# Loading and converting the first layer's weights earlier in a fused attention and two-layer expert kernel

## The chip, the cores and the metric

The kernel runs on one core of a Trainium2 chip. The time is device microseconds of one execution, and the result is the median of a few executions. Before the change it is 835.37 us (three runs, 835.11 to 836.59).

## What is computed

Three stages follow one another; 2176 tokens pass through all of them.

```python
# attention: 4 batches, 8 heads, 512 local and 32 global queries of 64 numbers
s_ll = where(abs(i - j) <= 32, scale * q_l @ k_l.T, -1e9)      # band of local keys
out_l = softmax([scale * q_l @ k_g.T, s_ll]) @ [v_g, v_l]
out_g = softmax(scale * q_g @ [k_g, k_l].T) @ [v_g, v_l]
x = [out_g, out_l] as rows of 512                               # 2176 x 512
# dense layer
h = x @ w_in                                                    # 512 x 2048
x = (h * sigmoid(h)) @ w_out                                    # 2048 x 512
# experts: tokens shared out over 8 experts by a capacity rule, then
out[mask] = relu(x[mask] @ w1[e]) @ w2[e]
```

The array w_in holds 64-bit floats. The kernel reads them as pairs of 32-bit words and makes 32-bit floats of them on the chip.

## The kernel before

The tokens are cut into six units (UNITS): the first has 256 tokens, the others 384. For units 0 to 3 the kernel computes attention and, mixed with it on TensorE, the matrix product with w_in of the unit whose attention is already done. Units 4 and 5 and the later stages come after that, and the change doesn't touch them.

**Attention** is a list of ticks (TICKS): a transpose of a chunk of keys (step_k, L250 and L256), of global rows (step_g, L262 to L267) or of queries (step_q, L250 and L272), a block of local attention (local, for batch b, query block qb and half hh of the heads, written (b, qb, hh) below), or global attention (glob). One call of piece() runs a tick, and with it the next stage of the attention blocks that are under way. A local block goes through scores on TensorE (L354, L359), row maxima on DVE (L371), exponentials on ACT (L378), transposes on TensorE (L385), a copy on ACT (L387), the product with V on TensorE (L392), scaling on DVE (L395), a transpose back on TensorE (L401), and then the two halves of x, the high part on ACT (L404) and the low part on DVE (L406).

**The weights** w_in come in 16 chunks of 128 columns, w0 to w15, 512 KB each (w_in_chunk, a generator that stops between its steps). A chunk is loaded by SP (L84). Its conversion takes two instructions on ACT (L68, L70), three on DVE (L72, L73, L74), one on POOL (L75), the cast of the high part on ACT (L94) and the low part on POOL (L96). All of these stand in the queues of engines that also serve attention, in program order. The class Line keeps the chunks: load() issues the next one's load, step() takes the chunks that are under way one step further and begins the next.

**The order** is set by hand in piece(). Each call adds a rate to wl, and chunks are loaded until the chunk count reaches wl; each call also adds a rate to acc[0], and for every whole unit there win.step() is called. Before unit 0's matrix product has begun (begun is empty) the rates are 0.26 and 0.25, from then on 0.4 and 0.4, and the steps only begin after four calls. Attention's own loads are issued in the order of the list LOADS by load_ahead(n), which runs up to six loads ahead of the ticks. Ahead of everything else load_ahead(6) issues the first six. Unit 0's matrix product (unit_dram, mm_h, L523) starts when both 128-token blocks of the unit are done, and the calls of piece() go on between its matmuls.

All loads named here are issued by SP on one queue, apart from the first batch's global rows, which ACT issues.

Of the kernel before, what the change touches and what calls it, by code (L numbers as in the profile page):

```python
# [27 lines left out]
def tile_kernel(ctx, tc, q_l, k_l, v_l, q_g, k_g, v_g, w_in, w_out, w_gate, w1, w2, out):  # L28
# [434 lines left out]
    def load_ahead(n):  # L463
        while loaded[0] < min(n, len(LOADS)):
            f, *a = LOADS[loaded[0]]
            uses = () if f == load_n and a[1] else USES[f]
            if any(free[u] < uses.count(u) for u in uses):
                return
            for u in uses:
                free[u] -= 1  # L470
            f(*a)
            loaded[0] += 1

    def owed():
        while acc[0] >= 1:
            acc[0] -= 1
            win.step()
# [29 lines left out]
    def ticks():  # L507
        for t in TICKS:

            while t[0] == "L" and through[0] < 2 and 4 * t[1] + t[2] >= 8 + 3 * through[0]:  # L510
                yield "wait"
            yield from tick(t)
        while live:
            yield from advance()
# [35 lines left out]

    T = ticks()
    win = Line()
    load_ahead(6)
    made = [0] * 16
    wl = -0.5
    done = 0
    acc = [0.0, 0.0]
    begun = []

    def piece():  # L560
        nonlocal done, wl
        if next(T, "end") in ("end", "wait"):
            return False
        done += 1
        if done > 4:
            acc[0] += 0.4 if begun else 0.25
            owed()
        wl += 0.4 if begun else 0.26
        while win.at < wl:
            win.load()  # L570
            if win.at == 16: wl = 0
        return True
# [4 lines left out]
    for u in range(RES[0]):  # L577
        while not ready(u):
            piece()
        if u == 0:  # L580
            win.have(0)
            begun.append(1)
        for i, _ in enumerate(unit_dram(u)):
            if u == 0 and i % 4 == 3 and i < 63:
                win.have(i // 4 + 1)
            acc[1] += 0.64 if u == 0 else 0.7
            while acc[1] >= 1 and piece():
                acc[1] -= 1
        through[0] += 1
    while piece():  # L590
        pass
# [702 lines left out]
    done = 0  # L1294
# [57 lines left out]
```

## Time and profile before

| | us |
|---|---|
| median of three runs | 835.37 |
| the profiled execution, its own time | 836.36 |
| its span, first to last instruction | 834.6 |
| TensorE (PE) busy in the span | 796.2 |
| DVE, ACT, POOL busy | 420.4, 391.6, 223.9 |

The profile is of a single execution, some 1 us above the median. PE is busy for 95% of the span, so over the whole kernel PE is what counts, and its 38 us of idle time are what a change of order alone can reach. The page's slices of 20.9 us show where PE isn't busy: in the first four it stands at 6, 6, 9 and 6 tenths, and in nearly all of the others at 9 tenths or more. The first four slices are attention of the first batch, with the conversion of w_in and unit 0's product in it.

### The profile page before, as it was taken

What the parts mean: (1) busy time and instruction counts of PE and PEld (TensorE: products, weight loads), DVE (VectorE), ACT (ScalarE), POOL (GpSimd) and SP (SyncE); (2) the same over time, 40 slices, a digit from 0 to 9 for tenths busy, and PEclk for the clock granted to TensorE, in tenths of its full rate; (3) what the DMA queues carried; (4) which work ended last, traced back from release to release, by engine and by line L of the source; (5) the groups of instructions that cost most, each with busy time, mean ns of one, the idle gap of its engine ahead of it and who ended that gap; (6) DMA issues with size and microseconds to landing.
All of it is one profiled execution on the core that took longest, in us unless ns stands there. A gap on an engine that the chain in (4) does not pass through costs nothing. (4 is left out here: it accounts for less than half of the span.)

```text
span 834.6 us, 18246 instructions
## 1 busy us (share of the span) xinstructions
PE 796.2 (95%) x7407; PEld 671.4 (80%) x7407; DVE 420.4 (50%) x923; ACT 391.6 (47%) x879; POOL 223.9 (27%) x209
## 2 busy tenths in 40 slices
PE   6696999999999999999999999999799999999997
PEld 4475778888888999976667777777589999999994
DVE  3789544544454356520004444566635666666650
ACT  3676544354453466636442434454225454544531
POOL 2456300000000046534243444343230211122001
PEclk9799899999999999999999999999899999999999
DMA  9957853882871443126642325445135656666511
GB/s 177 238 175 206 208 141 95 196 204 76 184 204 40 162 135 115 51 95 197 202 139 64 123 67 187 160 150 174 53 89 170 219 169 226 193 221 205 193 61 38
DMA packets 131687, 125.24 MB, mean 150 GB/s; under 512 B 64560, under 2 KB 100416, under 8 KB 131600
## 3 DMA queue, kind: packets, MB, share of 16 engines
q1 hardware_dynamic: 126912, 114.65, 48.2%
q0 software_dynamic: 2784, 8.93, 3.0%
q8 instruction: 60, 0.98, 0.5%
q10 hardware_dynamic: 1904, 0.46, 0.4%
q14 instruction: 27, 0.22, 0.1%
HBM read 92.68 MB, written 20.71 MB: 136 GB/s over the span
## 5 line engine op out<-in xcount | busy, mean ns | idle before, releaser
L1150 PE MATMUL acc<-w,ghi 128*128 128x512 f32 x544 | 179.6, 405 | 4.3 <-PEq L1034 4.3
L523 PE MATMUL S<-xhi,w 128*128 128x384 f32 (+1 forms) x512 | 167.2, 359 | 0.3 <-DMA h_d<-hs 0.3
L1150 PEld LDWEIGHTS acc<-w,ghi 128*128 128x128 f32 x544 | 101.4, 190 | 32.5 <-issue 11.9
L1150 PE MATMUL acc<-w,glo 128*128 128x512 f32 x272 | 109.8, 404 | 0.0
L1260 PE MATMUL h<-xshi,we 128*128 128x272 f32 x512 | 108.7, 292 | 0.0
L523 PEld LDWEIGHTS S<-xhi,w 128*128 128x128 f32 x512 | 95.4, 191 | 11.0 <-issue 5.5
L58 DVE TENSOR_TENSOR we<-eraw,we 128x1024 fp32r<-128x1024 f32 x64 | 79.8, 1247 | 28.3 <-ACT we L55 28.3
L1278 PE MATMUL acc<-hh,we 128*128 128x272 f32 x448 | 93.4, 288 | 0.0
L58 POOL TENSOR_TENSOR glo<-ht,ghi 128x512 fp32r<-128x512 f32 x44 | 61.8, 1416 | 95.8 <-ACT ghi L55 92.2
L523 PE MATMUL S<-xlo,w 128*128 128x384 f32 (+1 forms) x256 | 83.5, 326 | 1.6 <-DVE xlo L406 1.6
L1260 PEld LDWEIGHTS h<-xshi,we 128*128 128x128 f32 x512 | 84.2, 188 | 0.1
L1260 PE MATMUL h<-xslo,we 128*128 128x272 f32 x256 | 73.8, 288 | 0.0
L1278 PEld LDWEIGHTS acc<-hh,we 128*128 128x128 f32 x448 | 73.7, 188 | 0.0
L523 PE MATMUL h<-xhi,w 128*128 128x384 f32 x256 | 69.7, 341 | 0.7 <-DVE fold L604 0.7
L55 ACT CAST we<-eraw 128x1024 fp32r<-128x1024 f32 x64 | 66.8, 1044 | 0.0
L1264 ACT ACTIVATE hh<-h 128x272 fp32r<-128x272 f32 x64 | 25.4, 398 | 88.0 <-PE h L1260 87.3
L1278 PE MATMUL acc<-hl,we 128*128 128x272 f32 x224 | 64.5, 288 | 0.0
L1150 PEld LDWEIGHTS acc<-w,glo 128*128 128x128 f32 x272 | 51.6, 190 | 14.4 <-issue 2.8
L75 POOL TENSOR_TENSOR cvu<-cvu,cvv 128x512 int32<-128x512 int32 x32 | 41.0, 1283 | 81.3 <-DVE cvu L74 54.6
L1217 POOL DMA_INDIRECT out_dram<-orow,idx x17 | 17.1, 1006 | 158.2 <-DVE orow L1225 140.6
L1166 ACT COPY x<-acc 128x512 f32<-128x512 f32 x17 | 10.0, 587 | 92.6 <-PE acc L1150 91.8
L523 PEld LDWEIGHTS S<-xlo,w 128*128 128x128 f32 x256 | 49.3, 193 | 1.8 <-DVE xlo L406 1.8
(229 smaller groups left out, 1431.6 us busy)
## 6 DMA issues: line engine op xcount, KB each, us to landing
eraw<-in_moe_w_dram SPq DMA_DIRECT2D x64, 512.0 KB, 3.7
ht<-h_d SPq DMA_DIRECT2D x44, 256.0 KB, 3.5
h_d<-hs SPq DMA_DIRECT2D x24, 384.0 KB, 3.3
gh<-h_d SPq DMA_DIRECT2D x12, 768.0 KB, 4.6
w<-in_moe_w_in_dram SPq DMA_DIRECT2D x16, 512.0 KB, 5.4
wraw<-in_moe_w_out_dram SPq DMA_DIRECT2D x16, 512.0 KB, 3.6
V<-vn SPq DMA_DIRECT2D x24, 256.0 KB, 3.8
x_d<-x SPq DMA_DIRECT2D x17, 256.0 KB, 2.0
```

The source lines that it names most:

```text
L55: nc.scalar.copy(hi, src)
L58: eng_lo.tensor_tensor(lo, src, hi.bitcast(F32), op=OP.subtract)
L75: nc.gpsimd.tensor_tensor(u, u, v, op=OP.add)
L523: nc.tensor.matmul(ps[:, :n], a, x[:, cc, :n], start=k == 0, stop=k == 11)
L1150: nc.tensor.matmul(ps, a[:, f % 4], x, start=f == 0 and k == 0, stop=f == 15 and k == 2)
L1166: nc.scalar.copy(x2, ps)
L1217: nc.gpsimd.indirect_dma_start(out=out, out_offset=bass.IndirectOffsetOnAxis(ap=at, axis=0), in_=r[:n], in_offset=None)
L1260: nc.tensor.matmul(ps, a, XS[e][x][:, c, o], start=k == 0, stop=k == 11)
L1264: nc.scalar.activation(hh, ps, AF.Relu)
L1278: nc.tensor.matmul(ACC[i][d], a, x, start=f == 0 and k == 0, stop=f == 7 and k == 2)
```

## The change

The first chunk of w_in is loaded after four of attention's loads and not after six. The counter wl starts at 1.0 in place of -0.5, the steps begin after two calls of piece() and not after four, and the four rates go from 0.25, 0.26, 0.4 and 0.4 to 0.33, 0.32, 0.42 and 0.42.

```diff
     T = ticks()
     win = Line()
+    load_ahead(4)
+    win.load()
     load_ahead(6)
     made = [0] * 16
-    wl = -0.5
+    wl = 1.0
     done = 0
...
         done += 1
-        if done > 4:
-            acc[0] += 0.4 if begun else 0.25
+        if done > 2:
+            acc[0] += 0.42 if begun else 0.33
             owed()
-        wl += 0.4 if begun else 0.26
+        wl += 0.42 if begun else 0.32
         while win.at < wl:
             win.load()
```

What the instructions are stays the same, and on PE their order too. What moves are the 16 loads on SP and the steps of the conversions on ACT, DVE and POOL. Three places show how.

On SP, at the start of the program: raw are attention's keys (L165) and queries (L170), vn and V0, V1 its values, and w0, w1, ... the chunks. Before:

```order
L165 DMA raw_127<-in_k_l_dram 128x8x64
L165 DMA raw_129<-in_k_l_dram 128x8x64
L170 DMA raw_136<-in_q_l_dram 128x8x64
L189 DMA vn_138<-in_v_l_dram 128x8x64
L203 DMA V0_117<-in_v_l_dram 32x8x64 x3
L84 DMA w0_160<-in_moe_w_in_dram 128x4x256
L165 DMA raw_162<-in_k_l_dram 128x8x64
L170 DMA raw_172<-in_q_l_dram 128x8x64
L189 DMA vn_138<-in_v_l_dram 128x8x64
```

With the change:

```order
L165 DMA raw_127<-in_k_l_dram 128x8x64
L165 DMA raw_129<-in_k_l_dram 128x8x64
L170 DMA raw_136<-in_q_l_dram 128x8x64
L84 DMA w0_138<-in_moe_w_in_dram 128x4x256
L189 DMA vn_140<-in_v_l_dram 128x8x64
L203 DMA V0_117<-in_v_l_dram 32x8x64 x3
L84 DMA w1_156<-in_moe_w_in_dram 128x4x256
L165 DMA raw_164<-in_k_l_dram 128x8x64
L170 DMA raw_174<-in_q_l_dram 128x8x64
L84 DMA w2_183<-in_moe_w_in_dram 128x4x256
L189 DMA vn_140<-in_v_l_dram 128x8x64
```

The third chunk of keys now has two chunks of w_in ahead of it and not one, and the second load of values has three and not one. Further on, w3 and w4 stand where w1 and w2 stood.

On ACT, ahead of the exponentials of block (0, 1, 0), which are the two L378 rows. Before:

```order
L68 ACTIVATE cvu_321<-w1_246 128x512
L70 ACTIVATE cvv_322<-w1_246 128x512
L404 CAST xhi_313<-tp_373 128x2x128
L378 ACTIVATE P_365,su2_121<-S_345,st_366 128x128 x2
L378 ACTIVATE P_365,su2_121<-S_346,st_366 128x128 x2
L94 CAST w0_411<-cvu_267 128x512
```

With the change:

```order
L94 CAST w0_329<-cvu_250 128x512
L68 ACTIVATE cvu_335<-w2_183 128x512
L70 ACTIVATE cvv_336<-w2_183 128x512
L404 CAST xhi_325<-tp_387 128x2x128
L94 CAST w1_393<-cvu_298 128x512
L68 ACTIVATE cvu_399<-w3_263 128x512
L70 ACTIVATE cvv_400<-w3_263 128x512
L378 ACTIVATE P_381,su2_121<-S_361,st_382 128x128 x2
L378 ACTIVATE P_381,su2_121<-S_362,st_382 128x128 x2
```

The exponentials stood behind chunk w1's first step; now they stand behind w3's.

On DVE, around the second chunk of the second batch's keys (L256) and that batch's global rows (L264, L267). Before:

```order
L256 COPY kT_114<-tp_1150 128x4x2x2x32
L406 TENSOR_TENSOR xlo_744<-tp_1167,xhi_743 128x2x128
L395 TENSOR_TENSOR x_1195<-tp_1178,st_1024 128x256
L72 TENSOR_SCALAR cvu_1142<-cvu_1142 128x512
L73 TENSOR_SCALAR cvu_1142<-cvu_1142 128x512
L74 SCALAR_TENSOR_TENSOR cvu_1142<-w13_1050,cvu_1142 128x512
L264 COPY gT_1227<-tp_1222 128x256
L267 COPY kT_114<-gT_1227 128x4x8x32
L545 COPY hs_1165<-S_1158 128x2x128
L406 TENSOR_TENSOR xlo_744<-tp_1238,xhi_743 128x2x128
L72 TENSOR_SCALAR cvu_1204<-cvu_1204 128x512
```

With the change:

```order
L256 COPY kT_114<-tp_1174 128x4x2x2x32
L72 TENSOR_SCALAR cvu_1149<-cvu_1149 128x512
L73 TENSOR_SCALAR cvu_1149<-cvu_1149 128x512
L74 SCALAR_TENSOR_TENSOR cvu_1149<-w15_988,cvu_1149 128x512
L406 TENSOR_TENSOR xlo_783<-tp_1196,xhi_782 128x2x128
L395 TENSOR_TENSOR x_1224<-tp_1207,st_1063 128x256
L264 COPY gT_1248<-tp_1243 128x256
L267 COPY kT_114<-gT_1248 128x4x8x32
L545 COPY hs_1194<-S_1187 128x2x128
L406 TENSOR_TENSOR xlo_783<-tp_1259,xhi_782 128x2x128
L371 TENSOR_REDUCE st_1309<-S_1288 128x2
```

Thirteen conversions stood ahead of this L256 on DVE and three behind it; now fifteen stand ahead and one behind.

## Rows read from the trace of the kernel before

**Rows 1.** Stretches: length, PE, PEld, DVE, ACT, POOL busy, PEclk, DMA share, GB/s

```profile
0.00:20.00 20.00, 13.07 (x167) 9.18 (x168) 7.44 (x18) 7.93 (x24) 4.30 (x24) 1.00 1.02 178
20.00:40.00 20.00, 12.15 (x234) 8.64 (x231) 14.88 (x36) 12.70 (x41) 7.28 (x7) 0.83 1.14 247
40.00:60.00 20.00, 18.95 (x261) 14.62 (x260) 16.24 (x36) 14.73 (x39) 12.69 (x10) 0.91 0.52 148
60.00:80.00 20.00, 15.10 (x230) 12.46 (x229) 19.51 (x39) 13.33 (x40) 13.01 (x10) 1.00 0.75 213
80.00:100.00 20.00, 16.42 (x248) 13.92 (x247) 13.50 (x28) 10.21 (x31) 10.53 (x9) 0.83 0.88 211
100.00:140.00 40.00, 40.00 (x587) 32.51 (x587) 18.33 (x60) 18.49 (x69) 1.04 (x2) 1.00 0.52 133
```

**Rows 2.** Waits of PE, 20 to 100 us: total, times, longest (us)

```profile
PE S L359 <- ACT qT L272: 4.2, 2, 3.6
PE tp L385 <- ACT P L378: 3.2, 2, 3.0
PE tp L401 <- DVE x L395: 2.1, 3, 1.3
PE S L354 <- DVE xlo L339: 2.0, 1, 2.0
PE tp L262 <- DVE kT L256: 1.2, 1, 1.2
```

**Rows 3.** Timeline of ACT, 24 to 26 us: start, us, instruction, idle before

```profile
24.60 0.66 ACT L68 ACTIVATE cvu<-w 128x512 f32<-128x512 f32 x1 [4.75 <-DMA w<-in_moe_w_in_dram]
25.16 0.65 ACT L70 ACTIVATE cvv<-w 128x512 int32<-128x512 uint32 x1
25.70 0.36 ACT L404 CAST xhi<-tp 128x256 fp32r<-128x256 f32 x1
25.95 0.38 ACT L378 ACTIVATE P<-S,st 128x128 f32<-128x128 f32 x1
```

**Rows 4.** DMA issues from 20.0 to 20.2 us (chunk w2): size, us to landing

```profile
w<-in_moe_w_in_dram SPq DMA_DIRECT2D x1, 512.0 KB, 6.2
```

**Rows 5.** Timeline of PE, places where it waited

```profile
14.96 1.08 PE L250 MATMUL tp<-ident,raw 128*128 128x128 f32 x4 [1.36 <-DMA raw<-in_k_l_dram]
...
64.83 0.27 PE L354 MATMUL S<-mb,identb 128*128 128x256 bf16 x1 [2.01 <-DVE xlo L339]
...
78.56 0.46 PE L262 MATMUL tp<-ident,raw 64*128 64x64 f32 x4 [1.23 <-DVE kT L256]
...
85.47 1.11 PE L359 MATMUL S<-kT,qT 64*32 64x128 f32 x32 [3.58 <-ACT qT L272]
```

**Rows 6.** Timeline of DVE, 39 to 82 us

```profile
39.32 0.42 DVE L406 TENSOR_TENSOR xlo<-tp,xhi 128x256 fp32r<-128x256 f32 x1
...
77.82 0.68 DVE L256 COPY kT<-tp 128x512 f32<-128x512 f32 x1
...
79.08 0.52 DVE L72 TENSOR_SCALAR cvu<-cvu 128x512 f32<-128x512 f32 x1
...
81.68 0.42 DVE L264 COPY gT<-tp 128x256 f32<-128x256 f32 x1
```

**Rows 7.** Timeline of POOL at 82 us

```profile
81.90 1.26 POOL L75 TENSOR_TENSOR cvu<-cvu,cvv 128x512 int32<-128x512 int32 x1 [1.15 <-DVE cvu L74]
```

**Rows 8.** Timeline of ACT, 83 to 86 us

```profile
83.20 0.62 ACT L94 CAST w<-cvu 128x512 fp32r<-128x512 f32 x1 [1.81 <-POOL cvu L75]
...
84.85 0.57 ACT L272 ACTIVATE qT<-tp 128x512 f32<-128x512 f32 x1
```

**Rows 9.** Single microseconds, columns as in rows 1

```profile
64.00:65.00 1.00, 0.17 (x1) 0.00 (x0) 0.97 (x3) 1.00 (x7) 0.00 (x1) 1.00 1.11 302
84.00:85.00 1.00, 0.00 (x0) 0.00 (x0) 1.00 (x3) 1.00 (x3) 0.92 (x2) 0.68 0.52 125
90.00:91.00 1.00, 1.00 (x6) 1.00 (x6) 0.93 (x3) 0.00 (x0) 0.00 (x0) 0.50 1.06 242
```

## The prediction

> **What bounds the kernel now.** I read the busy time by stretch first, then the waits of PE, then the timelines around the longest of them. The stretches [rows 1] say where anything can be won. From 100 us to 140 us PE is busy all 40.00 us, and from there on it stays so but for the seams between stages. From 20 to 100 us it is busy for 62.6 us of 80 (12.15 + 18.95 + 15.10 + 16.42). DVE is busy for 16.24 of 20 us between 40 and 60 us, and for 19.51 of 20 between 60 and 80. So for 40 us the first unit's stage is bound by DVE, or by ACT and POOL where a conversion hands over to them, and PE waits for their results [rows 2]: 3.6 us in one piece for queries that ACT makes, 3.0 for exponentials, 2.0 before a local block's second score tile, 1.2 for keys. In no row of these waits is PE held by a chunk of w_in. The chunks come in time; what they do is stand in front of attention's work in the queues of ACT, DVE and POOL.
>
> The change leaves PE's instructions and their order as they are. The conversions are the same sixteen. So the whole effect is how much sooner or later PE gets through the attention that is mixed with unit 0's product, that is, through the last long wait, which ends at 85.47 us [rows 5]. From there on PE waits for nothing before 140 us worth counting, and a shift at this point reaches the end in full. The sum has three terms up to that point and one behind it.
>
> **Term 1, the loads: +3.5 us.** Up to 40 us the DMA engines are full: their share stands at 1.02 and 1.14 [rows 1]. Each chunk that is put ahead of attention's loads holds these back by its own length, 524 KB at the 178 or 247 GB/s of these two rows, 2.9 or 2.1 us. The first place where that shows is the third chunk of keys, for which PE waited 1.36 us up to 14.96 us [rows 5]: one more chunk lies ahead of it, so that wait grows by some 2 us. The second place takes that delay in and is longer. ACT stood idle for 4.75 us until w1 landed, at 24.60 us [rows 3], and block (0, 1, 0)'s exponentials came at 25.95. With the change w3 stands at this place. All that lay ahead of w2 in the old queue, and w2 itself, lies ahead of w3 in the new one. w2 was issued at 20.0 to 20.2 us and landed 6.2 us later [rows 4], at 26.3. One chunk more at 2.1 us gives 28.4. From the start of L68 to the next instruction behind L70 it is 1.10 us (24.60 to 25.70) [rows 3], so the exponentials start at 29.5, 3.5 us later than before. I take 247 GB/s, since it is the rate of the stretch in which w3 lands. The bounds: at 178 GB/s +4.4; with the extra chunk at no cost, 26.3 + 1.1 = 27.4, or +1.4. A gain is excluded, because w3 can't land before the bytes that were ahead of w2.
>
> The Trainium skill gives, on its page "DMA: Bandwidth & Descriptors", section "Anatomy of one DMA", a variable cost of bytes over 436 GB/s; by that a chunk would take an estimated 1.2 us and this term would be +2.6. The trace's full engines at 178 and 247 GB/s speak against that rate here.
>
> **Term 2, what DVE makes up: -2.8 us.** Block (0, 1)'s last low part (L406) ran at 39.32 us and the copy of the second batch's second chunk of keys (L256) at 77.82 [rows 6]. Ahead of that L406 DVE has now done six conversions and not four; ahead of that L256 fifteen and not thirteen. Between the two it is nine in either kernel, and the other work is the same, so the 3.5 us are carried along unless DVE's idle time shrinks. That is 3.76 us from 40 to 60 and 0.49 from 60 to 80 [rows 1], 4.25 in all, and it bounds the term from 0 to -4.25. Most of it lies soon after the restart, in waits for results of PE and ACT; with two chunks more in hand, some work is always ready there. I take two thirds, which puts L256 at 77.82 + 3.5 - 2.8 = 78.5 us.
>
> On this stretch a new wait appears. Ahead of the row maxima of block (0, 3, 0) DVE now does a conversion more. Its price is the one from 79.08 to 81.68 us, 2.6 us [rows 6], and PE's wait before L354 at 64.83, now 2.01 us [rows 5], grows by about that. PE gets it back before 78.56, where it waited 1.23 us for L256, and on the way, where it waited for x [rows 2]. So I cost it at nothing; uncovered it would be 2.6 us.
>
> **Term 3, the tail of the conversions: -1.25 us.** From L256 (77.82) to PE's L359 (85.47) it took 7.65 us. In between, ACT's cast of w13 (83.20) waited for POOL's step (81.90, 1.26 us), which waited for DVE, and w15's first step stood between that cast and the queries (84.85) [rows 6 to 8]. With the change only w15's conversion is left there. The chain is L256 0.68, a conversion on DVE 2.60, from its end to the cast 1.52 (81.68 to 83.20), the cast 0.62, a high part (L404) 0.36, and from the queries' start to L359 0.62 (84.85 to 85.47): 6.40 us. L359 comes at 78.5 + 6.4 = 84.9 us, 0.55 us earlier than before.
>
> **Term 4, the clock: -1.4 us.** The granted clock, 1.00 until 84 us, falls to 0.68 in the slice from 84 to 85 and stands at 0.50 until 91 [rows 9], which is the 1.2 GHz level. Behind the 2.01 us wait at 64.83 it stayed at 1.00 [rows 5, 9]; behind the 3.58 us wait it fell. PE worked from 85.47 to 91 at half speed, which cost (91 - 85.47) / 2 = 2.8 us. With the change the wait before L359 is split, a part of it lying before L401, and each part should be under 2 us. Then the clock stays up and 2.8 us are won. But the longer wait before L354 can bring a fall of its own. I take half.
>
> Sum: 3.5 - 2.8 - 1.25 - 1.4 = -1.95 us. The profiled execution would take 836.36 - 1.95 = 834.4; the median of the runs lies 1.0 us lower, so the forecast is **833.4 us**.
>
> **Rivals.**
> *Slower.* The loads cost term 1 and nothing is made up, since DVE was bound by the chain from ACT through POOL and not by its own work. It decides if L256 comes later than about 79.1 us (77.82 + 1.25): then L359 is late. With no idle time made up and the clock as before, +3.5 - 1.25 = +2.25, 837.6 us; at 178 GB/s 838.5. For it speaks that DVE is all but full from 60 to 80 us; against it the 3.76 us of idle time before.
> *No change.* The gains and the delay cancel. L359 comes 0.55 us earlier, and the half-speed stretch moves to the new wait before L354, its cost the same: 834.8 us. The Trainium skill says on "TensorE: Matmul & The Clock Gate", section "What's actually happening", that the low clock is the default and activity releases it; by that the fall follows the longest gap wherever it is put, and the time is this one. The trace agrees so far that the 3.58 us gap brought a fall and the 2.01 us gap none.
> *Twice the gain.* The early loads have room after all (term 1 at +1.4), DVE takes all of that in, and the clock stays up: 1.4 - 2.8 - 1.25 - 2.8 = -5.4, 829.9 us. Against it speak DMA shares above 1.
> That the change doesn't do what it says is excluded by the order of SP, ACT and DVE, which moved as described.
>
> **How the numbers follow.** The forecast gets 0.35, the slower rival 0.25, no change 0.23, the larger gain 0.17. What a measurement of this kernel can tell from no change is about 0.2%, 1.7 us, and the forecast lies just outside; I count 0.05 of its chance as no change. That makes 0.47 faster, 0.28 the same, 0.25 slower. The likeliest case alone, with term 4 between 0 and -2.8 and term 1 between +3.5 and +4.4, spans 832.0 to 835.7. The range that should hold 8 in 10 takes in most of the larger gain and the slower rival's first value: 829.5 to 838.0.
>
> **What would show it.** In the changed profile ACT's exponentials of block (0, 1, 0) start near 29.5 us, behind a wait for a chunk's load (term 1; if they start before 27 it is wrong). L256 of the second batch's second keys runs near 78.5 us (term 2). L359 of the second batch's first block starts near 84.9, with a wait of less than 2 us (term 3), and the granted clock stays above 0.5 from 84 to 91 us (term 4). PE waits over 4 us before L354 at about 69 us. Wrong would be a wait of PE for a chunk, or a change of PE's time behind 140 us.

## The result

The changed kernel takes 843.53 us (median of four runs, 840.93 to 844.90) beside 835.98 for the kernel before on the same chip: a ratio of 1.0083, 95% interval 1.0067 to 1.0099. It is some 7 us slower, where 2 us less were forecast. The profiled execution of the change is the lowest of its four, at 840.93 us (span 839.2); that of before is 836.36.

The stretches of the changed kernel (columns as in [rows 1]: length, PE, PEld, DVE, ACT, POOL busy, granted clock, DMA share, GB/s):

```profile
0.00:20.00 20.00, 11.00 (x130) 7.65 (x131) 7.76 (x17) 7.59 (x24) 4.30 (x24) 0.90 1.04 210
20.00:40.00 20.00, 12.54 (x250) 8.83 (x256) 17.76 (x37) 14.13 (x38) 11.52 (x9) 0.84 1.01 242
40.00:60.00 20.00, 17.29 (x246) 13.44 (x230) 17.99 (x37) 15.57 (x46) 12.53 (x11) 0.83 0.83 208
60.00:80.00 20.00, 14.63 (x206) 11.77 (x206) 17.08 (x32) 13.21 (x39) 12.80 (x10) 0.83 0.40 106
80.00:100.00 20.00, 16.18 (x218) 13.98 (x217) 11.15 (x27) 7.70 (x27) 7.46 (x6) 0.86 0.68 169
100.00:140.00 40.00, 40.00 (x588) 33.14 (x586) 16.76 (x53) 17.58 (x61) 1.04 (x2) 0.98 0.59 147
```

Beside [rows 1] PE has lost 2.07 us up to 20 us and 1.66 between 40 and 60. DVE's idle time from 40 to 80 us, which was to shrink from 4.25 us, is 4.93 (2.01 + 2.92).

PE's timeline, the places that answer to [rows 5] and two new ones:

```profile
16.70 1.08 PE L250 MATMUL tp<-ident,raw 128*128 128x128 f32 x4 [2.83 <-DMA raw<-in_k_l_dram]
...
71.37 0.37 PE L354 MATMUL S<-mb,identb 128*128 128x256 bf16 x1 [3.97 <-DVE xlo L339]
...
88.08 0.67 PE L359 MATMUL S<-kT,qT 64*32 64x128 f32 x32
...
95.02 1.11 PE L250 MATMUL tp<-ident,raw 128*128 128x128 f32 x4 [3.17 <-DMA raw<-in_k_l_dram]
...
101.28 0.60 PE L250 MATMUL tp<-ident,raw 128*128 128x128 f32 x4
```

The shift against before can be read off one instruction after the other: +1.74 at the keys (16.70), +6.54 at L354 (71.37), +2.61 at L359 (88.08). The 3.58 us wait before that L359 is gone. PE was done with its work at 95.02 - 3.17 = 91.85 us, where before the same L250 ran at 91.57 without a wait: **0.28 us late**. Then comes a wait that was not in the forecast, for the third chunk of the second batch's keys. The next L250 runs at 101.28 us, 6.26 late. That is the loss. The kernel before at the same two L250:

```profile
91.57 0.60 PE L250 MATMUL tp<-ident,raw 128*128 128x128 f32 x4
...
95.02 0.60 PE L250 MATMUL tp<-ident,raw 128*128 128x128 f32 x4
```

The granted clock in single microseconds (columns as above):

```profile
71.00:72.00 1.00, 0.63 (x17) 0.33 (x24) 0.94 (x5) 1.00 (x6) 0.00 (x0) 0.50 0.00 0
84.00:85.00 1.00, 1.00 (x10) 0.93 (x10) 0.97 (x2) 0.00 (x0) 0.18 (x1) 1.00 0.69 159
95.00:96.00 1.00, 0.98 (x5) 0.98 (x6) 0.00 (x0) 0.00 (x0) 0.00 (x0) 0.50 0.78 179
```

At 84 us it now stays at 2.4 GHz, where [rows 9] show the fall. But it is at 1.2 GHz from 71 to 77 us, behind the 3.97 us gap, and from 95 to 101, behind the 3.17 us gap. From the one L250 to the next it is 6.26 us (101.28 - 95.02), before 3.45 (95.02 - 91.57): the second stretch costs 2.8 us, and with the gap of 3.17 us that is the 6 us.

Why are the keys late? SP's timeline (SPq: issue of a DMA; start, us, line, destination and source):

```profile
73.45 0.37 SPq L548 DMA_DIRECT2D h_d<-hs  x1
...
81.73 0.37 SPq L548 DMA_DIRECT2D h_d<-hs  x1
82.14 1.34 SPq L189 DMA_DIRECT2D vn<-in_v_l_dram  x1
83.58 0.71 SPq L232 DMA_DIRECT2D V<-vn  x1
...
90.13 0.51 SPq L548 DMA_DIRECT2D h_d<-hs  x1
90.74 0.44 SPq L165 DMA_DIRECT2D raw<-in_k_l_dram  x1
```

The keys (L165) stand on SP behind nine copies into V, these behind a load of values (L189), and that behind a store of h (L548) that waits for DVE's copy L545. Before, the stores were issued at 66.92 and 74.78 us and the keys at 84.87:

```profile
74.78 0.37 SPq L548 DMA_DIRECT2D h_d<-hs  x1
...
84.87 0.44 SPq L165 DMA_DIRECT2D raw<-in_k_l_dram  x1
```

Now all is 6 to 7 us later. DVE's timeline shows where that begins:

```profile
67.38 0.75 DVE L371 TENSOR_REDUCE st<-S 128x2 f32<-128x256 f32 x2
...
72.97 0.42 DVE L545 COPY hs<-S 128x256 f32<-128x256 f32 x1
...
81.25 0.42 DVE L545 COPY hs<-S 128x256 f32<-128x256 f32 x1
81.86 0.66 DVE L256 COPY kT<-tp 128x512 f32<-128x512 f32 x1
```

The first row (L371) is the row maxima of block (0, 3, 0). Before:

```profile
61.33 0.73 DVE L371 TENSOR_REDUCE st<-S 128x2 f32<-128x256 f32 x2
```

Twelve conversions (L74) are now ahead of them, before nine. On ACT, fourteen conversions have been begun (L68) ahead of the block's exponentials, before eleven:

```profile
27.50 0.68 ACT L68 ACTIVATE cvu<-w 128x512 f32<-128x512 f32 x1 [1.69 <-DMA w<-in_moe_w_in_dram]
...
28.64 0.35 ACT L378 ACTIVATE P<-S,st 128x128 f32<-128x128 f32 x1
...
60.92 0.62 ACT L94 CAST w<-cvu 128x512 fp32r<-128x512 f32 x1 [0.40 <-POOL cvu L75]
...
65.06 0.62 ACT L94 CAST w<-cvu 128x512 fp32r<-128x512 f32 x1 [1.89 <-POOL cvu L75]
...
68.90 0.62 ACT L94 CAST w<-cvu 128x512 fp32r<-128x512 f32 x1 [1.71 <-POOL cvu L75]
69.42 0.66 ACT L68 ACTIVATE cvu<-w 128x512 f32<-128x512 f32 x1
...
70.53 0.35 ACT L378 ACTIVATE P<-S,st 128x128 f32<-128x128 f32 x1
```

The casts L94 follow each other at 4.1 and 3.8 us, each waiting for POOL's L75, and the exponentials stand behind the last. The profile puts PE's wait at 71.37 down to DVE's L339, which ends at 71.34 us; the second of the block's four exponentials ends at 71.32. It is the exponentials: PE goes on 0.8 us after the first of them has begun, in the change (70.53 and 71.37), before (64.00 and 64.83) and in the run *hold_maxima* below (72.45 and 73.30), where L339 is done 3.8 us earlier and the profile names them.

Far behind all this the profiled execution gets 1.7 us back, at a place that the change doesn't touch. Near 595 us PE waits in both kernels (4.26 us up to 594.14 before, 3.68 us up to 599.76 in the change) and the clock falls to 1.2 GHz. Single microseconds (columns as above), the kernel before and, apart, the change:

```profile
598.00:599.00 1.00, 1.00 (x4) 0.76 (x3) 0.90 (x5) 0.00 (x0) 0.00 (x0) 0.50 0.08 16
```

```profile
603.00:604.00 1.00, 1.00 (x6) 0.83 (x5) 0.90 (x6) 0.00 (x0) 0.00 (x0) 0.99 0.08 16
```

Before, the clock is low in seven slices from 593 to 600 us, here in four from 599 to 603. The profiles of *loads_only*, *steps_only* and *stores_half* (below) have the long stretch, those of *run_rate*, *late_rate* and *slow_rate* the short one. I take it as the luck of an execution, which makes the loss look smaller in this trace than in the medians.

### The profile page after: what moved, and what is told of

Same layout as the page of the kernel before. It is cut to its first block, busy times and chain, and to the rows that moved or that the text cites. A ratio compares the mean times of both kernels' runs of the same rounds, so it can differ in the third digit from the quotient of the medians.

```text
span 839.2 us, 18251 instructions
## 1 busy us (share of the span) xinstructions
PE 797.3 (95%) x7407; PEld 673.1 (80%) x7407; DVE 423.3 (50%) x923; ACT 392.3 (47%) x879; POOL 222.8 (27%) x209
## 5 line engine op out<-in xcount | busy, mean ns | idle before, releaser
L523 PE MATMUL S<-xhi,w 128*128 128x384 f32 (+1 forms) x512 | 168.9, 363 | 0.4 <-ACT xhi L404 0.4
L523 PEld LDWEIGHTS S<-xhi,w 128*128 128x128 f32 x512 | 97.2, 195 | 10.8 <-issue 5.5
L75 POOL TENSOR_TENSOR cvu<-cvu,cvv 128x512 int32<-128x512 int32 x32 | 41.1, 1284 | 75.4 <-DVE cvu L74 35.8
```

What stands on the lines that cost most here:

```text
L75: nc.gpsimd.tensor_tensor(u, u, v, op=OP.add)
L523: nc.tensor.matmul(ps[:, :n], a, x[:, cc, :n], start=k == 0, stop=k == 11)
```

## The experiments

All kernels compute the whole result. Ratios are against the kernel before, run beside them on the same chip, with the 95% interval.

**Loads alone, conversions alone.** *loads_only* has the load statements and load rates of the change and the old conversion rates. *steps_only* is the reverse.

```diff
 loads_only, against the change
-        if done > 2:
-            acc[0] += 0.42 if begun else 0.33
+        if done > 4:
+            acc[0] += 0.4 if begun else 0.25
 steps_only, against the kernel before
-        if done > 4:
-            acc[0] += 0.4 if begun else 0.25
+        if done > 2:
+            acc[0] += 0.42 if begun else 0.33
```

> The early and denser loads of the changed kernel, with the conversion order of the kernel before. Theory A (two causes in a chain: the loads set attention back by about 3 us at the restart; the denser conversions put further conversions ahead of block (0,3,0)'s row maxima, and that wait, the fall of the clock behind it and the late keys make up the rest): the restart (L406 of block (0,1)) comes near 43 us, the row maxima of (0,3,0) at 62 to 64, PE's wait before L354 stays under 2.5 us and the clock at 1.00 from 70 to 77 us, the third chunk of the second batch's keys is issued before 88 us and PE waits less than 1 us for it; the time is about 837.5 us. Theory L (the loads do all of it, the order of the conversions nothing): 843 us, with the 3 us wait for keys. Theory S (the denser conversions do all of it): 836 us.

> The denser conversions of the changed kernel, with the loads of the kernel before. Ten conversions stand ahead of block (0,3,0)'s row maxima (nine before, twelve in the changed kernel). Theory A: the restart as before, near 39 to 40 us, the row maxima near 64, a wait before L354 of 3 to 4 us with a fall of the clock behind it, the keys issued some 3 us later than before with a wait under 1 us; about 838 us. Theory L: 836 us. Theory S: 843 us.

*loads_only*: 835.40 us, 0.9995 (0.9984 to 1.0006). The early loads alone cost nothing and bring nothing that can be told from the noise. ACT's timeline of it at the place of [rows 3]:

```profile
24.68 0.37 ACT L378 ACTIVATE P<-S,st 128x128 f32<-128x128 f32 x1
```

The keys at 16.67 us are late as in the change (a wait of 3.35 us), but the exponentials of (0, 1, 0) come at 24.68 us, earlier than before (25.95), and L406 at 38.96 us. What holds them up in the change is not the load that lies ahead of w3 but that w3's conversion stands ahead of them on ACT (27.50 above). The old 3.58 us wait at L359 is there again, at 84.83 us.

*steps_only*: 844.81 us, 1.0112 (1.0098 to 1.0127). That is all of the loss and more, but it arises at another place. ACT's timeline of it:

```profile
24.71 0.66 ACT L68 ACTIVATE cvu<-w 128x512 f32<-128x512 f32 x1 [8.27 <-DMA w<-in_moe_w_in_dram]
...
25.81 0.57 ACT L387 COPY PT<-tp 128x512 f32<-128x512 f32 x1
```

Without the early load, w1's conversion stands at the head of ACT's queue for 8.27 us with attention behind it, and PE waits 7.34 us at L392. L406 of (0, 1) runs at 46.62 us, 7.30 late, and that is nearly all of the 8.18 us by which this execution is longer than that of before. So this run doesn't show how the change loses its time; it shows that the denser conversions need the early loads, which don't pay for themselves. Theories A and L are out by their times; S is nearest, without a mechanism so far.

**Two repairs of the symptom.** *k_mid* moves the late keys ahead of the copies into V; *hold_maxima* moves two conversions behind the row maxima of (0, 3, 0).

```diff
 k_mid, against the change
+    LOADS.remove((load_k, 1, 2))
+    LOADS.insert(LOADS.index((load_v, 1, 0)), (load_k, 1, 2))
+    need["L", 1, 0, 0] += 1
 hold_maxima, against the change
-            owed()
+            if not 34 < done <= 38: owed()
```

> The changed kernel with one load moved: the third chunk of the second batch's keys is issued ahead of the copies into V and the store that stood before it on SP's queue. Theory A: it is issued near 83 us and not at 90.7; the wait of 3.17 us at 95 us and the second stretch at half clock go (3.17 and some 3 us), and the wait before L354 stays at 4 us; about 837.5 us. Rival (the keys are only the first of several late loads; queries or V copies, all 6 us late on the same queue, hold PE in their place): a wait of 2 to 3 us at another instruction between 95 and 115 us, and 841 to 843 us.

*k_mid*: 846.52 us, 1.0133 (1.0109 to 1.0156). The keys are issued at 83.31 us and the wait for them is gone, as asked, but others stand in its place. PE's timeline:

```profile
96.10 1.41 PE L392 MATMUL tp<-V,PT 128*32 128x64 f32 x32 [1.93 <-DMA V<-gv]
...
108.45 0.27 PE L354 MATMUL S<-mb,identb 128*128 128x256 bf16 x1 [2.62 <-ACT hs L549]
```

The rival's mechanism holds, at more than its price of 841 to 843 us: everything on SP is late, and pulling one load forward pushes the copies into V back.

> The changed kernel with two conversions put behind block (0,3,0)'s row maxima and not ahead of them: ten stand ahead of them and not twelve; loads and all other positions as in the changed kernel. Theory A: the maxima come about 5 us earlier, near 62 us, PE's wait before L354 shrinks to 2 us or less, the clock stays at 1.00 there, the copies of h come 4 to 6 us earlier and with them the store and the keys, so the wait at 95 us goes too; about 837 us. Theory L (the restart's delay alone counts): the time stays at 843 us.

*hold_maxima*: 843.63 us, 1.0086 (1.0069 to 1.0103), no gain. The timeline of all engines:

```profile
62.26 0.76 DVE L371 TENSOR_REDUCE st<-S 128x2 f32<-128x256 f32 x2 [0.88 <-PE S L359]
...
67.45 0.62 ACT L94 CAST w<-cvu 128x512 fp32r<-128x512 f32 x1 [4.17 <-POOL cvu L75]
...
70.81 0.62 ACT L94 CAST w<-cvu 128x512 fp32r<-128x512 f32 x1 [1.52 <-POOL cvu L75]
...
72.45 0.35 ACT L378 ACTIVATE P<-S,st 128x128 f32<-128x128 f32 x1
...
73.30 0.37 PE L354 MATMUL S<-mb,identb 128*128 128x256 bf16 x1 [7.50 <-ACT P L378]
```

DVE's maxima came 5 us earlier, but the exponentials 2 us later, for on ACT the same casts stand ahead of them and wait for POOL, which waits for the conversions that DVE now does later. Here the profile names the exponentials as what ends PE's wait. That gave theory B: a conversion ahead of an attention instruction costs one step of the chain ACT, DVE, POOL, ACT, wherever DVE's own part of it stands.

**The two rates apart.** *run_rate* keeps the denser conversions up to the point at which the unit's product begins and has 0.4 behind it; *late_rate* has the old rate and threshold up to there and 0.42 behind it. Both have the early loads.

```diff
 run_rate, against the change
-            acc[0] += 0.42 if begun else 0.33
+            acc[0] += 0.4 if begun else 0.33
-        wl += 0.42 if begun else 0.32
+        wl += 0.4 if begun else 0.32
 late_rate, against the change
-        if done > 2:
-            acc[0] += 0.42 if begun else 0.33
+        if done > 4:
+            acc[0] += 0.42 if begun else 0.25
```

> The changed kernel with the old rates of 0.4 once the unit's product runs; only the rates before that point, the threshold and the loads stay changed. Theory B (a conversion that stands ahead of an attention instruction in the queues of ACT and DVE holds it back by one step of the conversions, some 3.9 us where they run back to back; the loads' order counts for nothing by itself): the restart (L406 of block (0,1)) comes near 43 us as in the changed kernel, since the same conversions stand ahead of it; thirteen starts of a conversion stand ahead of the exponentials of (0,3,0) on ACT (eleven before, fourteen in the changed kernel), so they come at 66 to 69 us; the keys are issued at 87 to 90 us; 840 to 842 us. Rival R (the rate of 0.42 while the product runs does it): 836 us.

> The changed kernel with the old threshold and the old rate of 0.25 up to the point at which the unit's product runs, and 0.42 from there on; the loads stay changed. Theory B: restart near 39 us as before, the exponentials of (0,3,0) near 63 us with as many conversions ahead of them as before, the keys issued near 84 us; 835.5 us. Rival R: 841 to 843 us.

*run_rate*: 840.95 us, 1.0056 (1.0041 to 1.0071), within what theory B gave: L406 of (0, 1) at 43.1 us, the keys issued at 88.66. PE gets back to 95.5 us at an L250 that ran at 95.02 before, and then loses 5 us at one place. The timeline of all engines:

```profile
99.35 1.44 SPq L165 DMA_DIRECT2D raw<-in_k_l_dram  x1
...
100.90 0.52 SPq L548 DMA_DIRECT2D h_d<-hs  x1
...
104.08 0.37 ACT L546 COPY hs<-S 128x256 f32<-128x256 f32 x1 [3.15 <-DMA h_d<-hs]
...
104.50 0.27 PE L354 MATMUL S<-mb,identb 128*128 128x256 bf16 x1 [3.14 <-ACT hs L546]
```

This is the other way in which the same queue stops PE: a store stands behind SP's copies into V and a load, its buffer hs (there are two) isn't free until it has landed, ACT's copy waits for the buffer, and PE for ACT. The rest of the 5 us is the clock, at 1.2 GHz from 105 to 108 us.

*late_rate*: 839.50 us, 1.0055 (1.0037 to 1.0073). Theory B's 835.5 was wrong here. The restart was early (L406 at 38.1 us), but one conversion more stood ahead of the attention between 65 and 90 us, and PE lost its time there in nine waits of at most 1.9 us and at 1.2 GHz (from 82 and from 89 us). A whole step is also too high a price: with the same loads, 11, 13 and 14 conversions begun ahead of the exponentials of (0, 3, 0) (*loads_only*, *run_rate*, the change) put them at 62.79, 68.00 and 70.53 us. That is some 2.6 us for each, where the casts lie 3.8 to 4.1 us apart.

**The stores off SP's queue.** In *stores_pool* POOL issues all of the first unit's stores of h, in *stores_half* those from the fourth on.

```diff
 stores_half, against the change (stores_pool without "and f >= 7")
-                    nc.sync.dma_start(h_d[:, t0:t0 + nt, f - 1:f + 1], hs[:, :nt])
+                    (nc.gpsimd if u == 0 and f >= 7 else nc.sync).dma_start(h_d[:, t0:t0 + nt, f - 1:f + 1], hs[:, :nt])
```

> The changed kernel with the first unit's stores of h issued by POOL and not by SP, so that no load of the second batch stands behind a store that waits for DVE's copy. If the late queue of SP is what turns a delay of some 0.3 us at 92 us into 6.3 at 107: the second batch's V copies and keys are issued by 82 us, PE waits for none of them at 95 us, the clock stays at 1.00 to 102 us, and the time is 836.5 to 838.5 us. Rival (DVE and ACT are late themselves, so PE would wait for x, hs or PT in place of the keys): 841 to 844 us. POOL's own waits could add 1 to 2 us to either.

> The changed kernel with the first unit's stores of h issued by POOL from the fourth one on (all of them did that in the run before, which cost POOL's conversions 1 to 2 us each up to 88 us). If SP's order is what turns the delay of 0.3 us at 92 us into 6.3 at 107: PE's L359 of the second batch's first block at 88 to 89.5 us as in the changed kernel, no wait for keys at 95 us, L250 at 107.5 us or earlier not later than 106, 837 to 839.5 us. Rival: 841 us, as with all stores on POOL.

*stores_pool*: 841.25 us, 1.0058 (1.0043 to 1.0074). No wait of PE behind 88.3 us any more, but PE gets there late (L359 at 92 us), since the stores stand between the conversions on POOL (0.73 to 0.94 us each).

*stores_half*: 838.38 us, 1.0032 (1.0018 to 1.0045), 4 to 5 us less than the change. It is the cleanest pair of the study: PE reaches L359 at 88.12 us, in the change at 88.08. SP issues the keys at 83.28 us and not at 90.74:

```profile
83.28 0.52 SPq L165 DMA_DIRECT2D raw<-in_k_l_dram  x1
```

PE's timeline:

```profile
88.12 0.67 PE L359 MATMUL S<-kT,qT 64*32 64x128 f32 x32
...
107.36 0.60 PE L250 MATMUL tp<-ident,raw 128*128 128x128 f32 x4
```

PE waits for nothing from 88 to 140 us, and the L250 that runs at 113.50 us in the change runs at 107.36 (before 107.23). The 6 us behind 88 us are SP's order. The profiled execution took 836.35 us, 2 us less than the median of the eleven and as long as that of before, so its trace doesn't show where the remaining 0.32% lie.

**The length of a step.** *lo_dve* (from *loads_only*), *after_lo_dve* and *before_lo_dve* let DVE, not POOL, subtract a chunk's low part (L96).

```diff
-        nc.gpsimd.tensor_tensor(t[:, 1], s, t[:, 0].bitcast(F32), op=OP.subtract)
+        nc.vector.tensor_tensor(t[:, 1], s, t[:, 0].bitcast(F32), op=OP.subtract)
```

> The early loads with the old conversion order (the run that stood level with the kernel before), and the low part of each chunk (L96) subtracted by DVE and not by POOL. If the step of a conversion is long because DVE's integer work runs beside POOL's L96 (L73 takes 0.43 us without it and 1.40 beside it): DVE's part of a conversion falls from some 3.5 us to some 2.5 with L96 in it, the casts L94 come less than 3.5 us apart, the second batch's keys (L256) come before 75 us and the time falls to 829 to 833 us. Rival (DVE's own work is the bound, and 0.7 us more for each of 16 conversions is added to it): 836 to 840 us.

> The changed kernel with the low part of each chunk (L96) subtracted by DVE and not by POOL. Theory B (a conversion that stands ahead of an attention instruction costs one step of the conversions, which is long because DVE's conversion work runs beside POOL's L96): the steps get shorter, casts L94 some 3.5 us apart, the three conversions more ahead of block (0,3,0) cost 1 to 2 us less in sum and the exponentials come at 68 to 69 us (70.5); 839 to 841 us. Rival (the loss comes from the positions alone, not from the step's length): 843 us or more.

> The kernel before with L96 on DVE alone. If the gain of the run with early loads and L96 on DVE came from L96: 833 to 834 us. If it needed the early loads: 836 us.

*lo_dve*: 833.17 us, 0.9965 (0.9954 to 0.9977): **faster than both kernels**, just above the 829 to 833 us expected, but its signs failed: casts 3.5 us apart at 58 to 62 us and not less, the second keys' L256 at 76.3 and not below 75. *before_lo_dve*: 835.73 us, 1.0001 (0.9989 to 1.0013). *after_lo_dve*: 841.39 us, 1.0070 (1.0052 to 1.0089), between what the two theories gave and within the intervals no better than the change (1.0083). So L96 on DVE gains with the early loads (0.35%), not without them; why the two go together was not traced further, and that a shorter step is what gains is not shown.

**The other way round.** If more conversions ahead of attention cost, fewer might gain. *slow_rate* is *loads_only* with 0.34 in place of 0.4 while the product runs; *slow_half* adds the store's edit, *slow_lo_dve* that of L96, *slow_half_lo_dve* both. *run_rate_half* is *run_rate* with the store's edit.

> The early loads with the old rates, but 0.34 and not 0.4 while the product runs: fewer conversions stand ahead of each attention instruction (eight and not nine ahead of the row maxima of (0,3,0)). Theory B, carried on to the other side: the maxima come at 57 to 58 us and the product still finds its chunks; 832 to 835 us. Rival (a conversion put later only delays the last ones, and the wait for queries at 85 us, which stands behind the last casts, grows): 836 to 840 us.

> The early loads, 0.34 while the product runs, stores of h from the fourth on issued by POOL. If the mechanism holds with its sign turned: the wait of 1.9 us before L354 at 100 us goes and the 3.5 us that PE was ahead at 88 us are kept, less what PE waits for low parts on POOL: 832 to 833.5 us. Rival (POOL, which already holds PE up with L96, is held up further by the stores): 835 to 838 us.

> The early loads, 0.34 while the product runs, L96 on DVE. PE's eight waits for L96 in the run without this (7.9 us in sum) go or move to DVE: 831 to 834 us. Rival (the late casts hold PE instead, or the store at 100 us takes the gain back as it did there): 835 us.

> Both: the early loads, 0.34 while the product runs, L96 on DVE, stores of h from the fourth on issued by POOL, which L96 no longer fills. If the mechanism holds, the gains add: 829 to 832 us. Rival (they meet at one later wait): 833 us, as with the early loads and L96 on DVE alone.

> The denser conversions only up to the point at which the product runs (as in the run with the old rate of 0.4 behind it, 0.56% slower), and the stores of h from the fourth on issued by POOL. If the two denser rates each hold a part of the remaining 0.32%: the wait of 3.14 us before L354 at 104 us goes, 836.5 to 837.5 us. If all of it sits in the early rate: 838 to 839 us. If the stores were not the mechanism: 841 us.

*slow_rate*: 835.47 us, 0.9995 (0.9981 to 1.0008). PE runs ahead (an L250 at 88.1 us that ran at 91.57 before), the maxima come at 57.6 us, but PE now waits for the chunks themselves, as no wait did before. The waits of PE from 40 to 110 us (total, times, longest):

```profile
PE S L523 <- POOL w L96: 6.5, 7, 1.7
```

Its lead is lost at 100 us, at a store of h on SP. Taking that away did not help: *slow_half* 837.13 us, 1.0021 (1.0004 to 1.0038), *slow_lo_dve* 836.43, 1.0006 (0.9994 to 1.0017), *slow_half_lo_dve* 835.15, 0.9987 (0.9972 to 1.0003). None brought the gain expected, and only the rival of *slow_half* (835 to 838 us) held. In all four PE waits for the low parts of the chunks (L96): 8.4, 3.8 and 5.6 us in sum from 40 to 110 us in the last three. That fewer conversions ahead of attention did not gain for this reason fits these waits; no run sets it apart.

*run_rate_half*: 838.25 us, 1.0022 (1.0012 to 1.0033). The wait at 104 us is gone, as expected, and 2.7 us of the loss with it; the 0.32% that *stores_half* leaves are, within the intervals, those of the early rate alone.

## Why the prediction was wrong

**Term 1, the loads.** +3.5 us at the exponentials of (0, 1, 0); they came at 28.64 us, +2.7. The size was near, within the bounds, and the wait for w3 is there. But it was put down to the loads. With the same loads and the old conversions there is no delay at all (*loads_only*). It is the denser conversions that set w3's conversion, and so w3's load, ahead of the exponentials.

**Term 2, what DVE makes up: the step that failed first.** -2.8 us forecast, bounds 0 to -4.25, +0.2 measured: L406 at 43.17 (+3.85), the L256 of the second keys at 81.86 us (+4.04) and not at 78.5. The text counted DVE's idle time as room. It did not shrink (4.93 us for 4.25). As I read the rows, that time is waiting inside the conversions' chain, and more conversions in hand don't fill it, since each begins on ACT behind the cast of another (casts 3.8 to 4.1 us apart). L256 came later than 79.1, the point from which the slower rival decides; its price, +2.25, lacked what follows.

**The conversion ahead of the row maxima, costed at nothing.** The wait before L354 was forecast as over 4 us and was 3.97. Its price was near: counted from L406 of (0, 1) it is one conversion more (six for five), and from there to the maxima it took 24.21 us (43.17 to 67.38), before 22.01 (39.32 to 61.33), 2.2 us more for 2.6. With the restart's +3.85, which nothing made up, L354 came 6.54 us late. The text asked only whether PE gets the time back. PE did, down to +2.61 at L359. DVE's copies of h did not in time (L545 at 81.25 us, before 74.30), and on them hang the stores and SP.

**Term 3, the tail.** 6.40 us from L256 to L359 forecast, 81.86 to 88.08 = 6.22 us measured. Right.

**Term 4, the clock.** Half of 2.8 us forecast. The stretch at 84 us is gone: from L359 until PE was ready for the late keys' L250 it took 3.77 us (88.08 to 91.85), before 6.10 (85.47 to 91.57), so 2.33 of the 2.8 us were won. The fall behind the longer wait before L354, which the text allowed for, came too; its cost is in the 2.61 us at L359.

**"From there on PE waits for nothing before 140 us worth counting."** This is the step that made the loss. It was read from the kernel before, where it is true, and no one asked what stands on SP behind the stores that wait for DVE. By the terms and L359 the change would have cost 0.28 us at 91.85; the wait for keys and the half clock behind it made 6.26 of it, shown by *stores_half*. "Wrong would be a change of PE's time behind 140 us" came up at 600 us, as 1.7 us the other way, by the clock; the loss lies ahead of 140 us.

Left open is how the two denser rates share the loss: the early one alone costs 0.56%, the late one 0.55%, both together 0.83%, in runs whose waits fall at different places.

## What to carry to other kernels

When an engine's results come later, ask which DMA issues wait for them and what loads stand behind those issues on the same queue; a store that waits holds every later load, and moving a single load out of it only chooses the next victim. Work that goes in steps through several in-order engines holds up the instructions behind it on each of them: here a conversion ahead of the exponentials cost some 2.6 us, putting DVE's part of two of them later gained nothing, and DVE's idle time made none of it up. Where a change has two parts, price each part without the other: here the loads were harmless, and the denser conversions on top of them were the cost.

## What was not expected of the hardware

The clock fell without a long gap. In *late_rate* PE's waits from 70 to 82 us were of 1.75, 0.36, 0.19, 0.17 and 1.91 us, none as long as the 2.01 us behind which it stayed up before [rows 5, 9], and yet the clock was at 1.2 GHz from 82 us (single microsecond, columns as above):

```profile
82.00:83.00 1.00, 1.00 (x6) 0.95 (x5) 0.96 (x3) 1.00 (x3) 0.92 (x2) 0.50 0.91 201
```

So term 4's reasoning, that a wait split into parts under 2 us keeps the clock up, doesn't hold.

DVE's conversion instructions take longer beside POOL's. The changed kernel's DVE and, apart, POOL:

```profile
62.45 0.43 DVE L73 TENSOR_SCALAR cvu<-cvu 128x512 int32<-128x512 int32 x1
...
65.34 1.39 DVE L73 TENSOR_SCALAR cvu<-cvu 128x512 int32<-128x512 int32 x1
```

```profile
64.98 1.47 POOL L96 TENSOR_TENSOR w<-cvu,w 128x512 fp32r<-128x512 f32 x1
```

The second L73 ends at 66.73 us, 0.28 behind the end of L96; with L96 on DVE (*lo_dve*) all sixteen L73 take 0.43 us. The Trainium skill says on "SBUF — State Buffer", section "Who interferes with whom", that DVE in its two-port mode and GpSimd contend for a pair of ports and the later one waits for the whole instruction of the other; the trace agrees, with 0.43 and 1.39 us, though no row shows the mode in which L73 runs.
